# A fused spectral layer and gated MLP: the scaling of the last two table groups given to ScalarE, and the two hand-written orders of the front replaced

## The chip, the cores and the metric

The kernel runs on one core of one Trainium2 chip. The metric is the device time of one execution in microseconds (us), the median over several runs. A profile is one execution seen by the hardware profiler; it counts from the first to the last instruction (the span), which is a little shorter than the device time.

The engines have their own instruction queues and run beside each other: TensorE (PE) multiplies, and its weight loads are listed apart as PEld; VectorE (DVE), ScalarE (ACT) and GpSimd (POOL) work on elements; SyncE (SP) mostly issues DMA transfers. An engine takes its instructions strictly in its program's order, so an instruction that waits for a semaphore holds up everything behind it on that engine.

## What is computed

```python
def _A_ref(x, w_r, w_i):
    X = rfft2(x.astype(float32), axes=(-2, -1))
    X = X * (w_r + 1j * w_i)
    return irfft2(X, s=(S, D), axes=(-2, -1)).astype(bfloat16)

def _B_ref(x, w_gate, w_up, w_down):
    return (gelu(x @ w_gate) * (x @ w_up)) @ w_down

h  = x + _A_ref(layernorm(x), w_r, w_i)      # x: 1 x 2048 x 576, bf16
h2 = h + _B_ref(layernorm(h), w_gate, w_up, w_down)   # F = 4608
```

A layer normalization, a two-dimensional Fourier filter with a residual, a second normalization, and an MLP with a tanh-approximated GELU gate, with a residual.

## The kernel before

**Tiling.** The 2048 tokens are 16 tiles of 128 (partition p, tile c is token 16p+c), each 576 wide, in the SBUF tensor `XO`. The Fourier transforms are matmuls with tables. There are four stages, one after the other in program order.

**Stage 1** (order string `SEQ1`, line 25; from the span's start to about 20 us). The tiles are in six groups, `GROUPS`: tiles 0-1, 2-3, 4-6, 7-9, 10-12, 13-15. For each group the kernel finds the reciprocal deviation of every token (`RS1`), multiplies it into the tables of the first transform (`ATS = ATB * RS1`, `ln1_scale`, line 519 on), and multiplies the tiles with the scaled tables on PE (`a_mm`, line 540 on, 9 matmuls a tile, 18 or 27 a group). A group's matmuls fill five PSUM banks, one after the other, of the eight, in rotation (`a_bank`); the results are copied to the bf16 tensor `U` (`a_ev`, line 556 on). Each word of `SEQ1` emits one step, the last letter being the engine (D = DVE, A = ACT, P = POOL):

- `B3`, `b3`: the two half-row statistics of tile 3 on DVE (L496). Tiles 3, 4 and 13 have their sums from ACT instead: `S` (sum, L488) and `Q` (squares, L492), with `m` a small product (L499).
- `v4`: variances of group 4 on DVE (L505, L508); `q4`: their square root on ACT (L512); `c4`: the reciprocal on DVE (L517), which completes `RS1` of the group.
- `x4`: the scaling of group 4's tables; on DVE one instruction a tile (L527), on POOL one a group (L522).
- `n4`, `t4`: a negated copy (`XN`, L569) and a rearranged tail (`XR`, L576) of the group's tiles, on POOL.
- `k104`: PE matmuls on zeros that only keep PE running (L538). `M4`: the group's matmuls (L553).
- `E22`: the copy of bank-full number 22 (group 22 // 5 = 4, its bank number 22 % 5 = 2 in time) from PSUM to `U` (L564). Bank-fulls named in a word with `F` are copied in two halves: `E` copies the first, which the second stage's first eight steps read, and `F` the second.

**Stage 2** (order string `SEQF`, line 29; about 20 to 47 us). For each of 16 frequency groups i: `Di` and `di` are 6 and 4 matmuls on `U` (L628), and `di`'s letter is the engine that copies the result to `CUS` (L618); `Bq` is 16 matmuls for two groups 2q and 2q+1 (L641); `bi` copies a group's result from PSUM to `YS` (L618); `Ti` multiplies it on DVE with the filter weights (L653), from `YS`, or, where `bi` and `Ti` end in x, from PSUM itself; `Vi` is 16 matmuls (L661) and a copy to `V` (L618); `Zi` gathers a 32-column remainder into `ZR` and `Rq` (8 matmuls, L676) treats the remainders of up to four groups, followed by two DVE instructions into `VR` (L680). A letter at the end of `Z` or `V` is the engine of the copy, ACT where there is none. PSUM is used as four pairs of banks, and `take` (line 600 on) gives each step the pair that has been free longest in the order of the string. So a matmul step waits for the copy that empties its pair.

**Stage 3** (order string `SEQ`, line 30; about 47 to 58 us): inverse transforms (L761, L804), the residual (L821), the second normalization (L828 to L848), transposes (L866) and the first three MLP blocks. It needs all of `V` and `VR`.

**Stage 4** is the MLP: four times 36 blocks of gate and up matmuls (L902, with GELU on ACT L910 and a product on DVE L911), followed by the down matmuls (L1003) and the sum with the residual (L1006). Ten tiles of the inverse transform are woven into the first down pass (L920 to L943).

`Prog.op` records each step with what it reads and writes, and `emit` turns the hazards into semaphore waits. Nothing reorders the steps: each engine's queue is the order of the strings. DMA loads are issued by SP in a fixed order (`LORD`, then the weights); POOL issues some of the MLP's.

Of the kernel before, what the change touches and what calls it, by code (L numbers as in the profile page):

```python
# [6 lines left out]
ACTF = mybir.ActivationFunctionType  # L7
# [14 lines left out]
PAUSE = 600  # L22
PARTS = ((0, 256), (256, 512))
GROUPS = ((0, 2), (2, 4), (4, 7), (7, 10), (10, 13), (13, 16))
SEQ1 = """b1 b0 B0 S3 B1 B2 b2 m3D Q3 v0 q0 c0 t1 v1 k14 q1 n0 S4 t0 Q4 x0D n1 c1 M0 E0D k104 b5 n2 m4P B6 B5 b6 x1P v2 E1A E2A M1 q2 t2 E3A B7 b7 c2 x2P E5A E4A B9 E8A n3 b9 b8 B8 b11 E9A E7A v3 E6A Q13 b14 b10 q3 S13 c3 k202 B11 n4 x3P M2 t3 E12A E11A B10 m13P b12 B12 E10A M3 v4 E14A B14 B15 q4 t4 c4 E13A x4D b15 E16A v5 t5 n5 E15A M4 E18A q5 E17A E19A c5 E20A E24A x5D E21D M5 E25D E23A E22A E26D F24D F26A F23A E28D E27D F28D E29A F25A F29A F22A F27D""".split()
LORD = "x0-2 x2-4 a0-4 x4-8 a4-8 x8-12 x12-16 a8-16".split()
SPLIT = tuple(int(w[1:-1]) for w in SEQ1 if w[0] == "F")
ACT_TILES = tuple(int(w[1:]) for w in SEQ1 if w[0] == "Q")
SEQF = """D1 D0 d1D d0 D3 D2 d3 B0 b0 b1D T1 d2 D4 T0 d4 D5 B1 D6 b2 d5 b3D d6 T3 Z0D V1 Z1P T2 B2 D7 b4 D8 b5 d7D d8 T4 V3 V0 B3 T5 b6 b7 V2 D10 Z2P Z3D Z4D D9 d10 d9 T6 D11 T7 Z5P R0 d11 R1 B4 D13 Z6P b8 T8 b9 Z7D d13 T9 B5 D12 b10 b11 Z8D V4D V5 d12 Z9P T10 R2 D14 D15 d14 V9 d15 Z10P B6 T11 b13D b12 V7 V6 T13 V8 B7 T12 b15 V10 b14x T14x Z11P V11 T15 Z12P V12 V13 Z13P Z14P R3 V14 V15 Z15P R4""".split()
SEQ = """I0 I1 N0 I2 N1 s0 I3 S1 N2 q0 c0 I4 n0 s2 e0 q1 N3 e1 n1 I5 c1 z0 s3 e2 n2 D1 N4 q2 c2 D2 n3 N5 g10 e3 g00 h10 z3 h00 g20 g11 h20 h11 g01 g21 h01 h21""".split()  # L30
QR0 = ((0, 2), (2, 3), (3, 4))
QR = QR0 + ((4, NPRE), (NPRE, 8), (8, 16))
# [294 lines left out]
def _build(nc, A_x, A_w_r, A_w_i, B_w_gate, B_w_up, B_w_down, out):  # L327
    P = Prog(nc)
    T = build_tables()
    dram = {n: nc.inline_tensor(_np_bf16(T[n]), name="c_" + n.lower()) for n in T}  # L330
    PE, DVE, ACT, SP, POOL = "pe", "dve", "act", "sp", "pool"
# [38 lines left out]
    RS1 = sb.alloc("RS1", [128, NT], F32)  # L370
# [30 lines left out]
    ATB = sb.alloc("ATB", [128, NT, 128], BF16)  # L401
    ATS = sb.alloc("ATS", [128, NT, 128], BF16)
# [44 lines left out]
    for i, w in enumerate(LORD):  # L447
        c0, c1 = (int(v) for v in w[1:].rstrip("@").split("-"))
# [46 lines left out]
    def ln1_half(c, h):  # L495
        P.op(DVE, lambda v: v.bn_stats(ST1[:, c, h, :], XO[:, c, 288 * h:288 * h + 288]), r=[("X", c)], w=[("ST1", c, h)])  # L496
# [22 lines left out]
    def ln1_scale(i, eng):  # L519
        c0, c1 = GROUPS[i]  # L520
        if eng == POOL:
            P.op(POOL, lambda g, c0=c0, c1=c1: g.tensor_tensor(ATS[:, c0:c1, :], ATB[:, c0:c1, :],  # L522
                                                               RS1[:, c0:c1].unsqueeze(2).to_broadcast([128, c1 - c0, 128]), op=ALU.mult),
                 r=[("RS1", i)] + [("ATB", c) for c in range(c0, c1)], w=[("ATS", c) for c in range(c0, c1)])
        else:
            for c in range(c0, c1):
                P.op(DVE, lambda v, c=c: v.tensor_scalar(ATS[:, c, :], ATB[:, c, :], RS1[:, c:c + 1], None, op0=ALU.mult),  # L527
                     r=[("RS1", i), ("ATB", c)], w=[("ATS", c)])
# [27 lines left out]
    def a_ev(n, eng, late=False):  # L556
        i, k = n // 5, AORD[n % 5]
        hs = (1,) if late else (0,) if n in SPLIT else (0, 1)
        g0, g1 = 8 * hs[0], 8 * hs[-1] + 8
        c0, c1 = GROUPS[i]  # L560
        m, b = c1 - c0, a_bank(i, k)
        src = bank(b, 0, 128, 0, 128 * m).rearrange("p (n g e) -> p n g e", n=m, g=64)[:, :, 4 * g0:4 * g1, :]
        dst = U[:, k, g0:g1, :, c0:c1, :].rearrange("p g s n e -> p n (g s) e")
        fn = (lambda v: v.tensor_copy(dst, src)) if eng == DVE else (lambda a: a.activation(dst, src, ACTF.Copy))  # L564
        P.op(eng, fn, r=[("PS", b)] + ([("EV", n)] if late else []), w=[("U", i, k, h) for h in hs] + ([] if late else [("EV", n)]))
# [11 lines left out]

    ENG = {"A": ACT, "D": DVE, "P": POOL}
    RUN1 = {"k": idle_mm, "S": act_sum, "Q": act_sq, "B": lambda c: ln1_half(c, 0), "b": lambda c: ln1_half(c, 1), "v": ln1_var, "q": ln1_sqrt, "c": ln1_rs, "M": a_mm, "x": ln1_scale, "E": a_ev, "F": lambda n, eng: a_ev(n, eng, True), "n": x_neg, "m": act_mean2, "t": x_tail}
    for w in SEQ1:  # L580
        a = w[1:]
# [3 lines left out]
    c = 0  # L585
    while c < NT:
        c1 = c + 1
        while c not in ACT_TILES and c1 < NT and c1 not in ACT_TILES:
# [3 lines left out]
             r=[(keys, k) for k in range(c, c1)], w=[("NM", k) for k in range(c, c1)])  # L592
        c = c1
# [152 lines left out]
    for t, w in enumerate(SEQ):  # L746
        k, i = w[0], int(w[1:])
# [326 lines left out]
```

## Time and profile before

| | |
|---|---|
| time, median of 3 runs | 490.08 us (489.91 to 490.16) |
| the profiled execution's own time | 489.97 us |
| its span, granted TensorE clock | 487.7 us, 1.000 |
| PE busy | 479.9 us, 98% of the span |
| DVE busy | 191.6 us, 39% |
| ACT busy | 147.0 us, 30% |
| POOL busy | 33.8 us, 7% |

The busy shares are means over stages that are limited by different things: PE alone counts in the long MLP, while in the first 57 us all engines are busy. The times of rows in the timeline and in the chain of waits are a start and a length in us from the span's start; "x3" is the number of instructions put into the row, and a bracket is the idle time of the engine ahead of it with what ended it. A length includes some latency that the next instruction of the same engine overlaps, so the distance from one start to the next is a little shorter than the length.

### The profile page before, as it was taken

The page shows a single profiled execution, that of the slowest core. Times are in us where ns is not written, and L with a number is a line of the kernel's source. Part 1 is how long each engine was busy: PE and PEld are TensorE (multiplying, and loading weights), DVE is VectorE, ACT ScalarE, POOL GpSimd, SP SyncE. Part 2 cuts the span into 40 slices and gives each one's busy share as a digit, 9 for nine tenths or more (in the row PEclk, how much of TensorE's full clock was granted, in tenths as well). Part 3 has the DMA queues.
Part 4 walks back from the last instruction along what each step waited for, and adds up shares of the span by engine and source line. Part 5 has one row for each costly group of instructions (what it writes and reads, how often), then busy time and mean ns, then how long its engine had stood idle before and what let it go on. Part 6 is the DMA issues. An engine that isn't in the chain of part 4 may idle for free.

```text
span 487.7 us, 10651 instructions
## 1 busy us (share of the span) xinstructions
PE 479.9 (98%) x4725; PEld 281.8 (58%) x4726; DVE 191.6 (39%) x382; ACT 147.0 (30%) x289; POOL 33.8 (7%) x66
## 2 busy tenths in 40 slices
PE   7899999999999999999999999999999999999998
PEld 3667744444688744444577644444677444444775
DVE  6888733433576534333311144333211233333111
ACT  6898733223222222233200022332100123323000
POOL 5412720000000010000000000000000000000000
DMA  8657999300001071100000001000000000000000
GB/s 281 156 146 223 316 354 370 103 13 1 1 22 38 16 234 23 23 1 1 0 19 20 13 21 23 13 1 1 7 19 18 7 1 1 1 1 1 13 18 19
DMA packets 26205, 31.03 MB, mean 64 GB/s; under 512 B 11792, under 2 KB 18320, under 8 KB 26160
## 3 DMA queue, kind: packets, MB, share of 16 engines
q1 hardware_dynamic: 23904, 21.07, 15.1%
q0 software_dynamic: 2256, 9.29, 5.4%
q8 instruction: 37, 0.61, 0.5%
q14 instruction: 8, 0.07, 0.0%
HBM read 26.02 MB, written 2.36 MB: 58 GB/s over the span
## 4 chain that ended last, share of the span: by engine, by line
PE 94%; DVE 3%; DMA 1%; POOL 0%; issue 0%; SPq 0%; ACT 0%; POOLq 0%; DVEq 0%
PE PS L902 57%; PE PS L1003 29%; PE PS L628 2%; PE PS L661 1%; DVE ST L496 1%; DMA XO<-in_A_x_dram 1%; PE PS L920 1%; PE PS L641 1%; DVE VR L680 1%; PE PS L938 1%; DVE XO L821 0%; PE PS L804 0%; PE PS L761 0%; DVE ATS L527 0%; SPq L237 0%
## 5 line engine op out<-in xcount | busy, mean ns | idle before, releaser
L902 PE MATMUL PS<-HT,WG 64*128 64x512 bf16 (+1 forms) x2160 | 228.7, 371 | 0.0
L902 PEld LDWEIGHTS PS<-HT,WG 64*128 64x128 bf16 x2160 | 105.0, 94 | 122.0 <-issue 0.9
L911 DVE TENSOR_TENSOR AT<-GL,PS 128x512 bf16<-128x512 bf16 (+1 forms) x147 | 99.4, 677 | 177.9 <-ACT GL L910 177.9
L910 ACT ACTIVATE GL<-PS 128x512 bf16<-128x512 f32 (+1 forms) x147 | 86.5, 588 | 262.9 <-PE PS L902 251.6
L1003 PE MATMUL PS<-WD,AT 128*128 128x288 bf16 (+2 forms) x1152 | 144.9, 286 | 0.0
L1003 PEld LDWEIGHTS PS<-WD,AT 128*128 128x128 bf16 x1152 | 110.7, 98 | 30.6 <-ACT GL L910 1.3
L902 PE MATMUL PS<-HT,WGX 64*128 64x512 bf16 x486 | 53.4, 376 | 0.0
L1006 DVE TENSOR_TENSOR OS<-PS,XO 128x288 bf16<-128x288 f32 (+2 forms) x32 | 14.6, 457 | 94.4 <-PE PS L1003 94.3
L902 PEld LDWEIGHTS PS<-HT,WGX 64*128 64x128 bf16 x486 | 23.7, 94 | 28.8
L628 PE MATMUL PS<-FT,U 64*128 64x288 bf16 x160 | 12.1, 284 | 0.4 <-ACT U L564 0.3
L925 ACT ACTIVATE EB<-PS 128x288 f32<-128x288 f32 x10 | 4.1, 410 | 27.7 <-PE PS L920 27.7
L553 PE MATMUL PS<-ATS,XO 128*128 128x128 bf16 x96 | 9.1, 220 | 2.6 <-POOL ATS L522 2.1
L653 DVE TENSOR_TENSOR TP<-YS,WS 128x1152 bf16<-128x1152 bf16 x15 | 11.0, 755 | 0.4 <-ACT YS L618 0.2
L496 DVE BATCH_NORM_STATS2 ST<-XO 128x6 f32<-128x288 bf16 x26 | 9.9, 441 | 2.3 <-DMA XO<-in_A_x_dram 2.3
L943 DVE TENSOR_TENSOR XO<-PS,XO 128x576 bf16<-128x576 f32 x10 | 7.6, 757 | 8.0 <-PE PS L938 8.0
L553 PEld LDWEIGHTS PS<-ATS,XO 128*128 128x128 bf16 x96 | 6.8, 98 | 4.9 <-POOL ATS L522 3.3
L931 DVE TENSOR_TENSOR QB<-PS,EB 128x288 f32<-128x288 f32 x20 | 8.2, 452 | 3.3 <-ACT EB L925 3.3
L848 DVE TENSOR_SCALAR HN<-XO,NM,RS 128x576 bf16<-128x576 bf16 (+1 forms) x28 | 9.3, 368 | 0.0
L564 ACT ACTIVATE U<-PS 128x384 bf16<-128x384 f32 (+2 forms) x29 | 9.2, 415 | 0.1
L618 ACT ACTIVATE CUS<-PS 128x576 bf16<-128x576 f32 x14 | 8.8, 657 | 1.4 <-PE PS L628 1.4
L628 PEld LDWEIGHTS PS<-FT,U 64*128 64x128 bf16 x160 | 6.4, 94 | 4.2 <-PE PS L628 0.7
L661 PE MATMUL PS<-VT,TP 64*128 64x128 bf16 x256 | 8.7, 217 | 0.1
(86 smaller groups left out, 203.1 us busy)
## 6 DMA issues: line engine op xcount, KB each, us to landing
WD<-in_B_w_down_dram POOLq DMA_DIRECT2D x9, 576.0 KB, 17.1
WG<-in_B_w_up_dram SPq DMA_DIRECT2D x3, 1152.0 KB, 12.7
WG<-in_B_w_gate_dram POOLq DMA_DIRECT2D x2, 1152.0 KB, 13.1
out_dram<-OS SPq DMA_DIRECT2D x30, 72.0 KB, 1.6
XO<-in_A_x_dram SPq DMA_DIRECT2D x3, 576.0 KB, 7.1
WG<-in_B_w_gate_dram SPq DMA_DIRECT2D x4, 288.0 KB, 3.8
WG<-in_B_w_up_dram SPq DMA_DIRECT2D x4, 288.0 KB, 3.7
WG<-in_B_w_gate_dram SPq DMA_DIRECT2D x1, 1152.0 KB, 9.6
```

Source lines behind the costliest of these rows:

```text
L496: P.op(DVE, lambda v: v.bn_stats(ST1[:, c, h, :], XO[:, c, 288 * h:288 * h + 288]), r=[("X", c)], w=[("ST1", c, h)])
L553: P.op(PE, lambda t, b=b, lhs=lhs, s=s, e=e, o=o, c=c: t.matmul(bank(b, 0, 128, o, o + 128), lhs, ATS[:, c, :], start=s, stop=e), r=[("X", ...
L564: fn = (lambda v: v.tensor_copy(dst, src)) if eng == DVE else (lambda a: a.activation(dst, src, ACTF.Copy))
L628: d_done[i, o] = P.op(PE, lambda t, b=b, us=us, h0=h0, o=o, s=(not second and j == 0), e=(second and j == 1): t.matmul(bank(b, 0, 128, 0, ...
L653: P.op(DVE, lambda v: v.tensor_tensor(TP[:, i % NP, :, :, :], y4, w4, op=ALU.mult), r=rk + wkeys[sum(i >= w[1] for w in WP)], w=[("T", i % ...
L661: P.op(PE, lambda t, c=c, h0=h0, h=h, k=k, vt=vt: t.matmul(bank(b + h, 0, 128, 128 * c, 128 * c + 128), TP[h0:h0 + 64, i % NP, k // 2, k % ...
L848: P.op(eng, lambda v, c=c, hs=hs, o0=o0, o1=o1, x0=x0, x1=x1: v.tensor_scalar(HN[:, hs, o0:o1], XO[:, c, x0:x1], NM[:, c:c + 1], RS2[:, c: ...
L902: op = P.op(PE, lambda t, h0=h0, kt=kt, wt=wt, b=b, s=(not second and j == 0), e=(second and j == n - 1): t.matmul(bank(b, 0, 128, c0, c1) ...
L910: P.op(ACT, lambda a: a.activation(GL[:, s2, c0:c1], bank(b0, 0, 128, c0, c1), ACTF.Gelu_apprx_tanh), r=[("PS", b0)], w=[("GL", s2)])
L911: P.op(DVE, lambda v: v.tensor_tensor(AT[:, f, c0:c1], GL[:, s2, c0:c1], bank(b0 + 1, 0, 128, c0, c1), op=ALU.mult), r=[("GL", s2), ("PS", ...
L1003: P.op(PE, lambda t, b=b, d0=d0, d1=d1, f=f, p=p: t.matmul(bank(b, 0, 128, 0, d1 - d0), AT[:, f, 128 * p:128 * p + 128], WD[:, f, d0:d1], ...
L1006: P.op(DVE, lambda v, b=b, d0=d0, d1=d1, p=p, c=c: v.tensor_tensor(OS[:, p % 2, d0:d1], bank(b, 0, 128, 0, d1 - d0), XO[:, c, d0:d1], op=A ...
```

## The change

Three things change, all of them ahead of stage 3. First, `ln1_scale` gets a branch for ScalarE (one activation a tile: a copy with `RS1` as the per-partition scale), and `SEQ1` uses it for groups 4 and 5, which DVE had (`x4D`, `x5D` become `x4A`, `x5A`); group 0 goes from DVE to GpSimd (`x0D` becomes `x0P`); groups 1 to 3 stay on GpSimd. Second, the copies of the bank-fulls are dealt out anew between ACT and DVE: DVE had nine (`E0`, `E21`, and seven halves) and now has twelve (`E14`, `E17`, `E18`, `E21`, and eight halves); ACT goes from 29 to 26. Third, the whole of both order strings is another order. In `SEQF` the copies of `d3`, `b4`, `V3`, `V8` go from ACT to DVE and those of `V4` and `b1` from DVE to ACT; `Z0`, `Z3`, `Z12` go to ACT, `Z1` to DVE, and `Z4`, `Z7`, `Z8` to GpSimd; `b14x`, `T14x` (the product from PSUM) become `b14`, `T14`. The lines behind line 525 move down by 4: L564 is L568 after the change, L628 is L632, and so on.

```diff
@@ -22,11 +22,11 @@
-SEQ1 =
-    b1 b0 B0 S3 B1 B2 b2 m3D Q3 v0 q0 c0 t1 v1 k14 q1 n0 S4 t0 Q4 x0D n1 c1 M0 E0D k104 b5 n2 m4P B6 B5 b6 x1P v2
-    E1A E2A M1 q2 t2 E3A B7 b7 c2 x2P E5A E4A B9 E8A n3 b9 b8 B8 b11 E9A E7A v3 E6A Q13 b14 b10 q3 S13 c3 k202 B11
-    n4 x3P M2 t3 E12A E11A B10 m13P b12 B12 E10A M3 v4 E14A B14 B15 q4 t4 c4 E13A x4D b15 E16A v5 t5 n5 E15A M4
-    E18A q5 E17A E19A c5 E20A E24A x5D E21D M5 E25D E23A E22A E26D F24D F26A F23A E28D E27D F28D E29A F25A F29A
-    F22A F27D
+SEQ1 =
+    S3 b0 B1 t1 B0 n0 b2 t0 b1 m3D v0 Q3 q0 B2 k14 c0 v1 q1 x0P M0 n1 E1A S4 c1 B5 Q4 b5 B6 k104 n2 m4P E2A b6 v2
+    b7 E0A x1P B7 q2 c2 B9 b8 M1 t2 B8 b9 v3 E5A E4A E3A x2P B11 E6A E7A B12 b10 E8A k202 M2 b11 S13 E11A q3 c3 n3
+    n4 E12A B10 b12 Q13 E10A x3P E9A t3 v4 B14 q4 b15 m13P c4 b14 t4 M3 B15 E13A v5 E15A x4A q5 E14D c5 E16A M4 t5
+    n5 x5A E17D E19A E20A E18D E24A E23D F23A E22A E21D M5 E25D E26D E27A E28D F24A E29D F26A F28D F29D F25A F22D
+    F27A
-SEQF =
-    D1 D0 d1D d0 D3 D2 d3 B0 b0 b1D T1 d2 D4 T0 d4 D5 B1 D6 b2 d5 b3D d6 T3 Z0D V1 Z1P T2 B2 D7 b4 D8 b5 d7D d8 T4
-    V3 V0 B3 T5 b6 b7 V2 D10 Z2P Z3D Z4D D9 d10 d9 T6 D11 T7 Z5P R0 d11 R1 B4 D13 Z6P b8 T8 b9 Z7D d13 T9 B5 D12
-    b10 b11 Z8D V4D V5 d12 Z9P T10 R2 D14 D15 d14 V9 d15 Z10P B6 T11 b13D b12 V7 V6 T13 V8 B7 T12 b15 V10 b14x
-    T14x Z11P V11 T15 Z12P V12 V13 Z13P Z14P R3 V14 V15 Z15P R4
+SEQF =
+    D0 D1 d0 d1D D2 D3 d2 d3D B0 D4 D5 b1 b0 T1 T0 d4 d5 B1 b2 b3D D6 T3 Z0 V0 d6 B2 D7 T2 b5 D8 b4D d7D d8 V2 V1
+    T5 Z1D B3 b7 T4 T7 Z2P D10 D9 b6 d10 d9 Z3 T6 V3D Z4P Z5P D11 Z6P R0 d11 V5 R1 B4 b8 T8 b9 Z7P T9 V4 B5 b10
+    D12 b11 T10 D13 Z8P d12 D14 d13 R2 d14 D15 Z9P d15 V10 B6 T11 b12 b13D V6 T12 V7 B7 T13 b14 Z10P b15 Z11P V8D
+    T14 Z12 V12 Z13P V9 V13 V11 T15 Z14P R3 V14 V15 Z15P R4
@@ -522,6 +522,10 @@
             P.op(POOL, lambda g, c0=c0, c1=c1: g.tensor_tensor(ATS[:, c0:c1, :], ATB[:, c0:c1, :],
                                                                RS1[:, c0:c1].unsqueeze(2).to_broadcast([128, c1 - c0, 128]), op=ALU.mult),
                  r=[("RS1", i)] + [("ATB", c) for c in range(c0, c1)], w=[("ATS", c) for c in range(c0, c1)])
+        elif eng == ACT:
+            for c in range(c0, c1):
+                P.op(ACT, lambda a, c=c: a.activation(ATS[:, c, :], ATB[:, c, :], ACTF.Copy, scale=RS1[:, c:c + 1]),
+                     r=[("RS1", i), ("ATB", c)], w=[("ATS", c)])
         else:
             for c in range(c0, c1):
                 P.op(DVE, lambda v, c=c: v.tensor_scalar(ATS[:, c, :], ATB[:, c, :], RS1[:, c:c + 1], None, op0=ALU.mult),
```

More of the change, by code (lines that the diff above doesn't have):

```diff
@@ L24 @@
 GROUPS = ((0, 2), (2, 4), (4, 7), (7, 10), (10, 13), (13, 16))
-SEQ1 = """b1 b0 B0 S3 B1 B2 b2 m3D Q3 v0 q0 c0 t1 v1 k14 q1 n0 S4 t0 Q4 x0D n1 c1 M0 E0D k104 b5 n2 m4P B6 B5 b6 x1P v2 E1A E2A M1 q2 t2 E3A B7 b7 c2 x2P E5A E4A B9 E8A n3 b9 b8 B8 b11 E9A E7A v3 E6A Q13 b14 b10 q3 S13 c3 k202 B11 n4 x3P M2 t3 E12A E11A B10 m13P b12 B12 E10A M3 v4 E14A B14 B15 q4 t4 c4 E13A x4D b15 E16A v5 t5 n5 E15A M4 E18A q5 E17A E19A c5 E20A E24A x5D E21D M5 E25D E23A E22A E26D F24D F26A F23A E28D E27D F28D E29A F25A F29A F22A F27D""".split()
+SEQ1 = """S3 b0 B1 t1 B0 n0 b2 t0 b1 m3D v0 Q3 q0 B2 k14 c0 v1 q1 x0P M0 n1 E1A S4 c1 B5 Q4 b5 B6 k104 n2 m4P E2A b6 v2 b7 E0A x1P B7 q2 c2 B9 b8 M1 t2 B8 b9 v3 E5A E4A E3A x2P B11 E6A E7A B12 b10 E8A k202 M2 b11 S13 E11A q3 c3 n3 n4 E12A B10 b12 Q13 E10A x3P E9A t3 v4 B14 q4 b15 m13P c4 b14 t4 M3 B15 E13A v5 E15A x4A q5 E14D c5 E16A M4 t5 n5 x5A E17D E19A E20A E18D E24A E23D F23A E22A E21D M5 E25D E26D E27A E28D F24A E29D F26A F28D F29D F25A F22D F27A""".split()
 LORD = "x0-2 x2-4 a0-4 x4-8 a4-8 x8-12 x12-16 a8-16".split()
@@ L28 @@
 ACT_TILES = tuple(int(w[1:]) for w in SEQ1 if w[0] == "Q")
-SEQF = """D1 D0 d1D d0 D3 D2 d3 B0 b0 b1D T1 d2 D4 T0 d4 D5 B1 D6 b2 d5 b3D d6 T3 Z0D V1 Z1P T2 B2 D7 b4 D8 b5 d7D d8 T4 V3 V0 B3 T5 b6 b7 V2 D10 Z2P Z3D Z4D D9 d10 d9 T6 D11 T7 Z5P R0 d11 R1 B4 D13 Z6P b8 T8 b9 Z7D d13 T9 B5 D12 b10 b11 Z8D V4D V5 d12 Z9P T10 R2 D14 D15 d14 V9 d15 Z10P B6 T11 b13D b12 V7 V6 T13 V8 B7 T12 b15 V10 b14x T14x Z11P V11 T15 Z12P V12 V13 Z13P Z14P R3 V14 V15 Z15P R4""".split()
+SEQF = """D0 D1 d0 d1D D2 D3 d2 d3D B0 D4 D5 b1 b0 T1 T0 d4 d5 B1 b2 b3D D6 T3 Z0 V0 d6 B2 D7 T2 b5 D8 b4D d7D d8 V2 V1 T5 Z1D B3 b7 T4 T7 Z2P D10 D9 b6 d10 d9 Z3 T6 V3D Z4P Z5P D11 Z6P R0 d11 V5 R1 B4 b8 T8 b9 Z7P T9 V4 B5 b10 D12 b11 T10 D13 Z8P d12 D14 d13 R2 d14 D15 Z9P d15 V10 B6 T11 b12 b13D V6 T12 V7 B7 T13 b14 Z10P b15 Z11P V8D T14 Z12 V12 Z13P V9 V13 V11 T15 Z14P R3 V14 V15 Z15P R4""".split()
 SEQ = """I0 I1 N0 I2 N1 s0 I3 S1 N2 q0 c0 I4 n0 s2 e0 q1 N3 e1 n1 I5 c1 z0 s3 e2 n2 D1 N4 q2 c2 D2 n3 N5 g10 e3 g00 h10 z3 h00 g20 g11 h20 h11 g01 g21 h01 h21""".split()
```

## Prediction

> **What bounds the kernel now.** I read the chain of waits first, in order of time, and its tail before its front.
>
> ```profile
> 20.47 2.40 PE PS L628 x36
> ...
> 47.24 1.03 PE PS L761 x7
> ...
> 55.72 1.63 PE PS L902 x28
> ...
> 57.74 68.58 PE PS L902 x674
> ...
> 450.04 35.40 PE PS L1003 x288
> ```
>
> From 57.74 on the chain is PE behind PE to the end, so the MLP is neither shortened nor lengthened here, and its matmuls follow each other without a gap. What the change can move is when the chain reaches 57.74. Stage 3 (47.24 to 57.74) keeps its order, so it moves as a block with the last L680 instruction, which ends at 47.2. Everything is decided in the two stretches ahead of it; the windows view gives their load.
>
> ```profile
> core 0: us, PE busy (x) PEld busy (x) DVE busy (x) ACT busy (x) POOL busy (x), PEclk, DMA share, GB/s
> 3.65:20.47 16.82, 13.88 (x159) 9.56 (x159) 15.73 (x65) 13.92 (x45) 11.39 (x23) 1.00 0.84 250
> 20.47:44.67 24.20, 23.98 (x552) 17.28 (x554) 20.38 (x37) 21.91 (x43) 4.29 (x10) 1.00 0.63 171
> ```
>
> In stage 1 DVE is busy 15.73 of 16.82 us and ACT 13.92 (94% and 83%): DVE is the fullest, ACT next. In stage 2 PE is busy 23.98 of 24.20 and ACT 21.91, so work given to ACT there has little room. A gain would be of the size of a us at most, 0.2% of the time; 0.2% (0.98 us) is also about what a measurement of this kernel can tell from no change.
>
> **Stage 1, step by step.** The walk below takes each engine's queue in the new order, the start-to-start distances of these rows, and the hops that they show.
>
> ```profile
> 9.05 0.61 POOL L522 TENSOR_TENSOR ATS<-ATB,RS 128x256 bf16<-128x256 bf16 x1
> ...
> 10.79 0.83 POOL L522 TENSOR_TENSOR ATS<-ATB,RS 128x384 bf16<-128x384 bf16 x1 [0.56 <-DVE RS L517]
> ...
> 13.76 0.83 POOL L522 TENSOR_TENSOR ATS<-ATB,RS 128x384 bf16<-128x384 bf16 x1 [0.17 <-POOL XN L569]
> ```
>
> ```profile
> 6.57 0.17 DVE L517 RECIPROCAL RS<-RS 128x2 f32<-128x2 f32 x1 [0.36 <-ACT RS L512]
> ...
> 10.49 0.16 DVE L517 RECIPROCAL RS<-RS 128x3 f32<-128x3 f32 x1
> 10.57 1.87 DVE L496 BATCH_NORM_STATS2 ST<-XO 128x6 f32<-128x288 bf16 x5
> ...
> 13.29 0.16 DVE L517 RECIPROCAL RS<-RS 128x3 f32<-128x3 f32 x1
> ...
> 15.99 0.83 DVE L527 TENSOR_SCALAR ATS<-ATB,RS 128x128 bf16<-128x128 bf16 x3
> ...
> 17.87 0.18 DVE L517 RECIPROCAL RS<-RS 128x3 f32<-128x3 f32 x1 [0.36 <-ACT RS L512]
> 18.08 0.58 DVE L527 TENSOR_SCALAR ATS<-ATB,RS 128x128 bf16<-128x128 bf16 x3
> ```
>
> ```profile
> 10.09 2.01 ACT L564 ACTIVATE U<-PS 128x256 bf16<-128x256 f32 x7
> 11.93 0.73 ACT L492 ACTIVATE JNK<-XO 128x576 bf16<-128x576 bf16 x1
> ...
> 13.59 1.62 ACT L564 ACTIVATE U<-PS 128x384 bf16<-128x384 f32 x4
> ...
> 17.54 0.30 ACT L512 ACTIVATE RS<-MV,EPT 128x3 f32<-128x3 f32 x1 [0.56 <-DVE MV L508]
> 17.74 3.48 ACT L564 ACTIVATE U<-PS 128x384 bf16<-128x384 f32 x12
> ...
> 50.14 0.77 ACT L795 ACTIVATE OS<-XO,NM 128x576 bf16<-128x576 bf16 x1
> ```
>
> ```profile
> 7.16 0.23 PE L553 MATMUL PS<-ATS,XO 128*128 128x128 bf16 x1 [0.26 <-DVE ATS L527]
> ...
> 9.72 0.23 PE L553 MATMUL PS<-ATS,XO 128*128 128x128 bf16 x1 [0.47 <-POOL ATS L522]
> ...
> 14.65 0.23 PE L553 MATMUL PS<-ATS,XO 128*128 128x128 bf16 x1 [1.30 <-POOL ATS L522]
> ...
> 19.79 0.39 PE L553 MATMUL PS<-ATS,XO 128*128 128x128 bf16 x4
> ```
>
> *Removed from DVE*: two scalings of group 0 and one copy of it (0.34 net), 0.83 for group 4 and 0.58 for group 5. *Added to DVE*: three full copies (`E14`, `E17`, `E18`) and one half more, all behind the last statistics.
>
> *Group 0.* One statistic (1.87 / 5 = 0.36 in distance) now stands behind the group's variances, so its reciprocal, at 6.57 before, comes at 6.21. GpSimd starts 0.14 behind the reciprocal's end and takes 0.61: 6.52 to 7.13, and PE starts at 7.19 (7.16 before). Nothing gained or lost.
>
> *What stands behind it on GpSimd*: `n1`, `n2`, `m4`, `x1`. They move back by 0.61 and a gap of 0.15, less idle time; `x1` starts at 9.47 (9.05), M1 at 10.14 (9.72), and ScalarE, whose next copy now needs M1, idles from 10.19 to 10.58. `x2` is cheap: it had 0.56 idle ahead of it, and with `t2` ending at 10.65 it starts at 10.8, as before.
>
> *Reciprocals of groups 2 and 3.* ScalarE now copies `E1` before it reads tile 4, so the squares that DVE needs are done at 9.6, and DVE idles 0.3; the reciprocal of group 2 comes at 10.44 (10.49). Between it and group 3's there are now eight statistics where there were seven, so that comes at 13.67 (13.29). Hence `x3` at 13.97 (13.76) and M3 at 14.86 (14.65).
>
> *The new scalings.* No row shows ScalarE on a 128-wide SBUF tile with a per-partition operand. Its nearest rows are 0.30 for 3 elements and 0.77 for 576 (L512 and L795, both with such an operand). On the line between them 128 elements take 0.40, and as the next instruction overlaps 0.10 (17.54 + 0.30 against the start at 17.74), some 0.31 lie from start to start. The ends are 0.20 (what the three-element row leaves, 17.54 to 17.74) and 0.40 (no overlap). I take 0.31, the line between its two rows: 0.93 a group, 1.86 in all, where DVE gave 1.41. The Trainium skill, "ScalarE: Activation LUTs", section "Rules for kernel authors", says to do a multiplication on VectorE and not on ScalarE; section "What ACT_TABLE_LOAD costs" has 186 ns + 93 ns for the operand + 0.833 ns an element, 93 ns of it overlapped, 0.29 a tile by an estimate from that, which would make the sum 0.1 less; no run here shows it yet.
>
> *ScalarE's queue* is then full. From 10.58: six 256-wide copies (0.263 apart: seven of them stand between 10.09 and 11.93), the sum of tile 13 (0.66), `E11`, square root 3, `E12`, squares of 13, `E10`, `E9`, square root 4, `E13`, `E15` (0.39 for each 384-wide one, 0.20 for a root) give 16.12. `x4`: 16.12 to 17.05. Root 5 and `E16`: 17.64. `x5`: 18.57. So group 4's third tile is ready at 17.14 (DVE: 16.82), group 5's at 18.66 (18.66): the earlier last reciprocal (17.39, before 17.87) is spent in ScalarE's queue: behind `x4`, which itself waits behind `E15` for PE, stand root 5, `E16` and `x5`, and for these wait DVE's reciprocal and M5. M5, 27 matmuls behind that tile and behind the copies that empty its banks, ends at 20.17 (20.18): no change.
>
> *The tail of the copies.* Behind `x5` ScalarE has `E19`, `E20` (0.79) and eight halves.
>
> ```profile
> 19.77 1.45 ACT L564 ACTIVATE U<-PS 128x192 bf16<-128x192 f32 x6
> ```
>
> At 0.23 each (1.45 less the last one's overlap, over six), `F24`, the fourth from the end, ends at 20.6, `F25` at 21.07. They free PSUM banks 1 and 2. In the new order the second matmul of `D0` writes bank 1 and the first of `D1` bank 2, so `D1` starts at 21.13. Before, the second D step began at 20.47 + 0.39 = 20.86, with 2.40 / 36 for a matmul. **Stage 1 costs 0.27 us.** Below, with 0.20 a scaling, it gains 0.4; with 0.40 it costs 0.8.
>
> **Stage 2.** The matmuls are the same 584. I walked the new order with 0.39 for a D step, 0.25 for d, 0.62 for B, 0.45 for V, and copies as below.
>
> ```profile
> 22.79 0.68 PE L641 MATMUL PS<-CUS,BT 64*64 64x288 bf16 x16
> 23.41 1.64 PE L628 MATMUL PS<-FT,U 64*128 64x288 bf16 x20
> ...
> 39.48 0.80 PE L641 MATMUL PS<-CUS,BT 64*64 64x288 bf16 x16
> ...
> 42.38 2.02 PE L661 MATMUL PS<-VT,TP 64*128 64x128 bf16 x64
> ```
>
> ```profile
> 32.43 1.76 ACT L618 ACTIVATE CUS<-PS 128x576 bf16<-128x576 f32 x3
> ...
> 43.13 3.07 ACT L618 ACTIVATE V<-PS 128x512 bf16<-128x512 f32 x6
> ```
>
> ```profile
> 41.19 1.43 DVE L653 TENSOR_TENSOR TP<-YS,WS 128x1152 bf16<-128x1152 bf16 x2
> 42.54 1.35 DVE L653 TENSOR_TENSOR TP<-PS,WS 128x1152 bf16<-128x1152 f32 x1
> ...
> 44.66 2.52 DVE L680 TENSOR_TENSOR VR<-PS,MK 128x512 bf16<-128x512 f32 x4
> ```
>
> ACT has 0.55 between 576-wide copies and 0.50 between 512-wide ones, and a dependent engine starts 0.1 to 0.17 behind an end. Two `B` steps mark the way: the first starts at 23.30 (22.79 before; D2 and d2 now stand ahead of it, so 0.25 of that is order), the seventh at 39.9 (39.48, with the same number of D and V steps ahead). The shift stays between 0.25 and 0.6, because ScalarE's load (22 us in 24) and the bank pairs hold PE to the same pace. The end gains a little: `T14` no longer reads PSUM (1.35 becomes 0.75), though `V8`'s copy (0.69) joins DVE's queue just ahead of it, and the last four DVE products run in the same 3.4 us. The last L680 ends at 47.38 (47.19): **0.2 us later in all**; stage 2 gives 0.1 back.
>
> The cover of what I put at nothing: the weight loads of the MLP. SP's order is unchanged, GpSimd's weight transfers stand behind the same last `Z15`, and the one PE instruction that it waits for before the first up weights is again in the middle of a V step (`V7` instead of `V6`, both behind `B6`).
>
> ```profile
> 41.26 4.48 SPq L237 DMA_DIRECT2D WG<-in_B_w_up_dram  x5
> ```
>
> ```profile
> WG<-in_B_w_up_dram SPq DMA_DIRECT2D x4, 288.0 KB, 3.7
> ```
>
> Issued by 45.74 and landing 3.7 later, they are there by 50, over 5 us before the first gate matmuls at 55.72.
>
> **The sum**: profiled execution 489.97 + 0.2 = 490.2; the median of the runs is 0.1 above that execution, so 490.3.
>
> **The rivals.**
>
> *Faster: DVE's relief counts in full.* If a scaling on ScalarE is 0.20 and ScalarE's copies start a few tenths earlier than I walked, M5 ends 0.6 sooner, at 19.6, and the last half copies with it; D1 then starts at 20.4, 0.45 early. If stage 2 also keeps the 0.67 that DVE loses on `T14`, the sum is 490.1 - 1.1 = 489.0. For it: DVE is the fullest engine of stage 1, its last reciprocal surely comes earlier, and half of the chain's pieces there are DVE's. Against it: ScalarE gets 1.86 us and has 16.82 - 13.92 = 2.9 to spare, most of it at moments when it has nothing ready.
>
> *Slower: ScalarE becomes the bound of stage 1.* Its queue has no idle time from 10.58 to the end; `x4` stands behind `E15`, and square root 5, which group 5 waits for, behind `x4`. Each 0.1 more for a scaling is 0.6 in the tail copies and in the first D steps. At 0.40 with a M1 that is another 0.2 late, stage 1 costs 1.0, and stage 2, with ScalarE the fullest engine next to PE, gives nothing back and loses 0.2 at bank pairs: 491.3. It decides from a scaling of about 0.38. The rule of the skill quoted above points here.
>
> *No effect at all*: that the front's time is hidden behind a weight load. The loads land 5 us early, so I give this nothing beyond the forecast's own middle.
>
> **How the numbers follow.** The forecast (both engines' changes cancel, 489.1 to 491.0) has 0.57; faster by over 0.2% has 0.17; slower by over 0.2% 0.26, more than faster since ScalarE's queue has no slack and the walk already ends late. The range of 8 in 10 runs from the faster case to the slower one: 489.0 to 491.4.
>
> **What would show it.** ScalarE's L527 rows at 0.40 each, 0.93 for three; the last reciprocal at 17.4; GpSimd's first L522 at 6.5 and the second at 9.5; M3's first matmul at 14.9; the first L632 matmuls (L628 before) from 20.4 with a stall for a U copy of ScalarE, 36 of them until 23.3; the last L684 ending at 47.4; the MLP's unbroken stretch from 57.9. A last L684 before 46.4 would make the prediction wrong, and show that stage 2 is paced by DVE; one behind 48.2 that ScalarE holds the front.

## The result, and the profile after

| | before | after |
|---|---|---|
| time, median of 21 runs each | 489.95 us (489.77 to 490.67) | 489.20 us (489.08 to 489.52) |
| ratio, with its 95% interval | | 0.9984 [0.9977, 0.9990] |
| the profiled execution's own time, its span | 489.97, 487.7 | 489.13, 487.3 |
| time outside the span | 2.24 | 1.80 |

The change makes the kernel 0.75 us faster, 0.16%: less than the 0.2% that the prediction took as the least that can be told, and yet told, since 21 runs give an interval that leaves out 1. The forecast was 0.2 us slower. The last row of the table is the mean, over the runs, of the time less the span of the same run (for the kernel before it was 2.22 to 2.24 in each batch of the experiments). It splits the gain: 0.3 us lie within the span (median 487.4, before 487.7), **0.44 us lie outside it**, in a place for which the prediction has no term at all.

The chain of waits of the changed kernel, in order of time (start, length, engine and line; lines behind 525 are 4 higher than before):

```profile
13.80 0.84 POOL ATS L522
...
14.69 1.68 PE PS L557 x27
...
16.39 0.28 PE PS L557 x2
...
16.68 0.28 PE PS L557 x2
...
16.96 3.07 PE PS L557 x50
...
20.27 2.71 PE PS L632 x39
...
22.98 0.61 PE PS L645 x16
...
42.29 0.65 ACT YS L622
...
43.14 2.94 ACT V L622 x6
...
46.21 1.68 PE PS L765 x12
...
57.37 68.58 PE PS L906 x674
```

Two things differ from the chain before. In stage 1 it ran through VectorE's statistics, scalings and copies, and two copies on ScalarE, until 20.47; at the end of stage 2 it ran through VectorE's last four products (L680). Its rows before the change:

```profile
18.08 0.58 DVE ATS L527 x3
18.66 1.09 DVE U L564 x3
19.77 0.56 ACT U L564 x2
...
46.62 0.57 DVE VR L680
```

Now stage 1 is PE behind PE from M3's start at 14.69 on, because the scalings of groups 4 and 5 are there, or nearly there, when PE comes to them: PE's weight loads wait 0.17 to 0.19 for each of group 4's three tiles (two matmuls to a tile in the rows at 16.39 and 16.68), and for group 5's the waits list none.

At the end of stage 2 the chain runs through ScalarE's last six copies of `V`, by a thin margin: five matmuls wait for these copies and start at 46.21, and when they are through, at some 46.85, VectorE's products have just ended too (44.33 + 2.47 = 46.80).

```profile
44.33 2.47 DVE L684 TENSOR_TENSOR VR<-PS,MK 128x512 bf16<-128x512 f32 x4
...
46.86 0.30 PE L765 MATMUL PS<-DT,VR 128*128 128x288 bf16 x1
```

The MLP's unbroken stretch starts at 57.37 (57.74), and nothing changes behind that.

The windows of stages 1 and 2 (busy time of PE, PEld, DVE, ACT, POOL):

```profile
3.65:20.47 16.82, 14.47 (x163) 9.85 (x161) 15.16 (x59) 14.53 (x50) 11.92 (x24) 1.00 0.79 244
20.47:44.67 24.20, 24.13 (x561) 17.43 (x559) 21.29 (x35) 21.70 (x43) 5.34 (x12) 1.00 0.60 175
```

VectorE gives 0.57 in stage 1, ScalarE takes 0.61 more, and PE, with 14.47 for 13.88, is done with more of its work by 20.47. The timelines of single engines show the steps that the prediction walked. VectorE's last two reciprocals, of groups 4 and 5:

```profile
15.31 0.18 DVE L517 RECIPROCAL RS<-RS 128x3 f32<-128x3 f32 x1
...
17.13 0.18 DVE L517 RECIPROCAL RS<-RS 128x3 f32<-128x3 f32 x1
```

ScalarE's two groups of scalings and the tail of its copies:

```profile
15.84 1.06 ACT L527 ACTIVATE ATS<-ATB,RS 128x128 bf16<-128x128 bf16 x3
16.71 0.38 ACT L512 ACTIVATE RS<-MV,EPT 128x3 f32<-128x3 f32 x1
16.90 0.58 ACT L568 ACTIVATE U<-PS 128x384 bf16<-128x384 f32 x1
17.34 1.00 ACT L527 ACTIVATE ATS<-ATB,RS 128x128 bf16<-128x128 bf16 x3
18.23 2.66 ACT L568 ACTIVATE U<-PS 128x384 bf16<-128x384 f32 x10
```

Three scalings take 0.87 from start to start (15.84 to 16.71) and 0.89 (17.34 to 18.23), 0.29 each. The weight loads of the first D steps:

```profile
19.96 0.09 PEld L632 LDWEIGHTS PS<-FT,U 64*128 64x128 bf16 x1
20.27 2.41 PEld L632 LDWEIGHTS PS<-FT,U 64*128 64x128 bf16 x39 [0.22 <-ACT U L568]
```

D starts at 19.96 (20.47), and its second matmul waits 0.22 for a copy of `U` on ScalarE.

### The profile page after: what moved, and what is told of

Same layout as the page of the kernel before. It is cut to its first block, busy times and chain, and to the rows that moved or that the text cites. A ratio compares the mean times of both kernels' runs of the same rounds, so it can differ in the third digit from the quotient of the medians.

```text
span 487.3 us, 10655 instructions
## 1 busy us (share of the span) xinstructions
PE 480.2 (99%) x4726; PEld 281.7 (58%) x4726; DVE 191.7 (39%) x375; ACT 147.4 (30%) x294; POOL 35.2 (7%) x68
## 4 chain that ended last, share of the span: by engine, by line
PE 96%; DVE 2%; ACT 1%; issue 0%; POOL 0%; POOLq 0%; DVEq 0%
PE PS L906 58%; PE PS L1007 29%; PE PS L632 2%; PE PS L542 1%; PE PS L557 1%; PE PS L924 1%; PE PS L645 1%; DVE ST L496 1%; PE PS L665 1%; ACT V L622 1%; PE PS L942 1%; PE PS L765 0%; DVE XO L825 0%; PE PS L808 0%; PE PS L870 0%
## 5 line engine op out<-in xcount | busy, mean ns | idle before, releaser
L632 PE MATMUL PS<-FT,U 64*128 64x288 bf16 x160 | 12.2, 284 | 0.1
L568 ACT ACTIVATE U<-PS 128x256 bf16<-128x256 f32 (+2 forms) x26 | 8.9, 449 | 1.2 <-PE PS L557 1.2
L542 PE MATMUL PS<-ZD 128*128 128x512 bf16 x20 | 7.4, 537 | 1.5 <-POOL ZD L430 1.5
L632 PEld LDWEIGHTS PS<-FT,U 64*128 64x128 bf16 x160 | 6.4, 94 | 4.2 <-ACT CUS L622 0.7
```

Source lines behind the costliest of these rows:

```text
L542: P.op(PE, lambda t: t.matmul(bank(b), ZD[:, 0:128], ZD[:, :], start=True, stop=True), r=["ZD"], w=[("PS", b)])
L632: d_done[i, o] = P.op(PE, lambda t, b=b, us=us, h0=h0, o=o, s=(not second and j == 0), e=(second and j == 1): t.matmul(bank(b, 0, 128, 0, ...
```

## The experiments

Each was timed in five rounds on the chip, with the kernel before beside it (489.93 to 490.02 in the five batches). "Span" is the median over a kernel's runs, "outside" the mean of time less span, and VectorE's count is the one of the profile page.

| kernel | time | span | outside | VectorE's count |
|---|---|---|---|---|
| before, with the branch unused (c0_control) | 489.97 | 487.7 | 2.23 | 382 |
| after | 489.20 | 487.4 | 1.80 | 375 |
| new `SEQ1`, old `SEQF` (s1_seq1_new) | 489.47 | 487.7 | 1.79 | 377 |
| old `SEQ1`, new `SEQF` (s2_seqf_new) | 489.62 | 487.5 | 2.12 | 380 |
| after, groups 4 and 5 on VectorE (x45d_new_order) | 490.61 | 488.6 | 2.03 | 381 |
| before, groups 4 and 5 on ScalarE (x45_old_order) | 491.33 | 489.5 | 1.80 | 376 |
| after, group 0 on VectorE (x0d_new_order) | 489.33 | 487.5 | 1.82 | 377 |
| after, group 3 on VectorE (after_x3_vector) | 489.77 | 487.9 | 1.82 | 378 |
| after, 0.28 us more in ScalarE's queue (x5_twice) | 489.48 | 487.7 | 1.80 | 375 |
| after, tail copies in another order (tail_swapped) | 489.20 | 487.4 | 1.81 | 375 |
| after, T14 from PSUM (after_t14_from_psum) | 490.57 | 488.8 | 1.79 | 375 |
| before, T14 in two steps (before_t14_two_step) | 491.07 | 488.9 | 2.14 | 382 |
| before, six VectorE memsets fewer (before_six_fewer_dve) | 489.49 | 487.6 | 1.87 | 376 |
| before, two VectorE memsets fewer (before_three_fewer_dve) | 489.81 | 487.7 | 2.10 | 380 |
| after, eight VectorE memsets more (after_eight_more_dve) | 489.66 | 487.5 | 2.15 | 383 |
| after, 32 VectorE memsets more (after_32_more_dve) | 489.29 | 487.5 | 1.81 | 407 |
| after, eight ScalarE instructions more (after_eight_more_act) | 489.22 | 487.4 | 1.81 | 375 |

**The theory at the start**: the new orders gain by taking the last scalings off VectorE. **Its rivals**: the gain is stage 2's alone, or it is no matter of the schedule at all.

### Which string carries it

```diff
 c0_control:   the branch of ln1_scale added, both strings as before
 s1_seq1_new:  SEQ1 as after, SEQF as before
 s2_seqf_new:  SEQ1 as before, SEQF as after
```

> The kernel before with the new branch of ln1_scale in the source and unused: the same instructions in the same order, four source lines lower. Both theories: 489.95 +- 0.15 us, ratio 1.000. It asks something else: the profiled executions differ by 0.84 us in time (489.97, 489.13) but by 0.4 in span (487.7, 487.3), so 0.4 lies outside the span. If that is a chance of the one execution of before, this kernel's executions have spans near 488.1 and 1.85 us outside; if it belongs to the kernel, spans near 487.7 and 2.25 us outside.

> The new SEQ1 (with ScalarE's scalings) and the old SEQF. Theory A (stage 2's order gave most of the gain: in the traces the first D step starts 0.5 earlier but the stalls behind it leave 0.12 of stage 1's gain, and 0.26 comes from stage 2): time 489.8 us, and the last L684 ends at 47.1. Theory B (stage 1 gave it all, stage 2's order only passes it on): 489.2 us, last L684 at 46.8.

> The old SEQ1 and the new SEQF. Theory A (stage 2's order is itself 0.26 us shorter, above all by the product T14 that no longer reads PSUM): 489.6 us, last L684 near 46.9. Theory B (stage 2's order only fits the new end of stage 1): 489.95 us or slower, since D0 and D1 then write the banks whose copies come last in the old order (up to 490.3).

The control has ratio 0.9999 [0.9991, 1.0008] and the same 2.23 outside: that part belongs to a kernel and not to chance. The new `SEQ1` alone gives 0.9991 [0.9982, 0.9999], nearly all of it outside: the last L684 ends at 47.10 as theory A had it (before: 47.18), and the time is lower than its 489.8 because of the part outside, which neither theory counted. Its chain of waits still ends stage 2 in VectorE:

```profile
22.84 0.61 PE PS L645 x16
...
44.64 0.69 DVE VR L684
```

The new `SEQF` alone gives 0.9994 [0.9985, 1.0003], by itself not told from no change, at theory A's 489.6; its chain passes through ScalarE's copies, as in the changed kernel:

```profile
43.35 2.94 ACT V L622 x6
...
57.57 68.58 PE PS L906 x674
```

So the shift of the chain at the end of stage 2 is `SEQF`'s work, worth 0.2 us of span. The two gains, 0.49 and 0.34, add up to about the 0.75 of both. Within the span the new `SEQ1`, with its scalings taken off VectorE, gives nothing that can be told beside the old `SEQF` (487.7) and 0.1 beside the new (487.5 to 487.4). That leaves little of the theory at the start: 0.44 of the 0.75 lies outside the span, and 0.2 is stage 2's.

### The scalings, in the new order and in the old

```diff
 x45d_new_order (from after):
-x4A ... x5A
+x4D ... x5D
 x45_old_order (from before):
-x4D ... x5D
+x4A ... x5A
 x0d_new_order (from after):
-x0P
+x0D
```

> The new orders with groups 4 and 5 scaled by VectorE (x4D, x5D) at the same places of the string. Theory A (the move to ScalarE is worth nothing by itself, the orders are): 489.2 +- 0.2 us. Theory B (the move relieves VectorE, which is the fullest engine of stage 1): VectorE has 1.4 us more behind its reciprocals, of which the copies E17, E18, E23, E21 behind them are late: M5's banks come free 0.5 to 1 late, 490.0 us.

> The kernel before with its own orders, and only the scalings of groups 4 and 5 given to ScalarE. Theory 'the new orders are what makes room for them': ScalarE's old queue has no room, B's first step comes 0.3 to 0.9 later than 22.79, 490.2 to 490.8. Rival 'the relief of VectorE pays by itself': B's first step up to 0.5 earlier, 489.4 to 489.8. VectorE's count falls only by what the scalings take away, so outside the span 2.0 to 2.24.

> The changed kernel with group 0's scalings back on VectorE. Theory 'giving group 0 to POOL frees VectorE for the later groups, and only the last third of a chain decides': VectorE is 0.5 us later from there on, D's first step 0.2 to 0.5 later than 19.96, 489.3 to 489.6. Rival 'ScalarE paces stage 1 from 10.6 on, VectorE has slack': 489.2, no change.

In the new order, VectorE in place of ScalarE costs 1.2 us of span: 1.0013 [1.0004, 1.0023] of before, in theory B's direction and nearly twice its size. VectorE's timeline there shows why: the last reciprocal, which stood at 17.13, comes at 18.11, behind group 4's scalings, and D starts at 21.15 (19.96).

```profile
16.50 1.24 DVE L531 TENSOR_SCALAR ATS<-ATB,RS 128x128 bf16<-128x128 bf16 x3
...
18.11 0.16 DVE L517 RECIPROCAL RS<-RS 128x3 f32<-128x3 f32 x1
```

In the old order, the same edit the other way costs 1.8 us of span: 1.0028 [1.0017, 1.0038], more than the 490.2 to 490.8 that the first theory had. There ScalarE's timeline has four copies between square root 5 and `x5`, which starts only at 19.47 (17.34 in the changed kernel), and M5 waits 1.36 for it:

```profile
17.96 0.29 ACT L512 ACTIVATE RS<-MV,EPT 128x3 f32<-128x3 f32 x1
18.15 1.47 ACT L568 ACTIVATE U<-PS 128x384 bf16<-128x384 f32 x4
19.47 1.01 ACT L527 ACTIVATE ATS<-ATB,RS 128x128 bf16<-128x128 bf16 x3
```

So the engine of the scalings and the order belong together: each undone alone is worse than both kernels. Group 0's engine hardly matters: 489.33, with a spread of runs (488.97 to 489.65) that covers 489.20 and does not decide between the two expectations.

### Is there slack left in stage 1?

```diff
 x5_twice (from after), behind the scalings of group 5 on ScalarE:
+for c in range(c0, c1):
+    activation(TM[:, 1, c:c+1], ATB[:, c, 0:1], Copy)
 tail_swapped (from after):
-E27A E28D F24A E29D F26A F28D F29D F25A
+F24A E27A E28D E29D F25A F28D F29D F26A
 after_x3_vector (from after):
-x3P
+x3D
```

> The changed kernel with three tiny ScalarE instructions more (some 0.2 to 0.3 us each) behind group 5's scalings. Theory 'ScalarE's queue is full to the end of stage 1, each us in it is a us of the span': 0.6 to 0.8 slower, 489.8 to 490.0. Rival 'B's first step waits for VectorE's or TensorE's work there': within 0.2 of 489.2.

> The changed kernel with ScalarE's tail copies in another order (each F half ahead of the E half before it). Theory 'D's eight steps, which start at 19.96 and last 3.02, wait for the banks that those F halves fill': the stretch shortens by 0.1 to 0.3, 488.9 to 489.1. Rival 'they wait for the last copy of all, whatever its place': 489.2, or up to 0.2 more where an E half comes late.

> The changed kernel with group 3's scalings on VectorE (three of some 0.2 to 0.25 us, M3 can start after the first) in place of POOL's one of 0.83. M3 starts some 0.7 earlier than 14.69, and VectorE is 0.6 to 0.75 later with the statistics and reciprocals of groups 4 and 5. Theory 'from M3's start on TensorE is the pace': D's first step and the end 0.3 to 0.7 earlier, 488.5 to 488.9. Rival 'TensorE only waits less where VectorE and ScalarE just keep up, so that the later statistics come back as a wait ahead of M4 or M5': 489.2 to 489.8. VectorE then has 378 instructions on the page, so outside the span 1.8 to 2.1.

The label x5_twice promises more than the edit does: the three instructions took 0.28 of ScalarE's queue, from 18.31 to 18.59, not the 0.6 to 0.8 that the expectation worked with.

```profile
18.31 0.38 ACT L531 ACTIVATE TM<-ATB 128x1 f32<-128x1 bf16 x3
18.59 2.64 ACT L571 ACTIVATE U<-PS 128x384 bf16<-128x384 f32 x10
```

They cost 0.28 (489.48 against 489.20), more than the rival's 0.2: at this place ScalarE has no slack, and what is put into its queue is added to the time. `tail_swapped` (`F24` one place earlier, `F25` and `F26` exchanged) gives 489.20, no change, as its rival had it. The wait ahead of the second D matmul gets shorter by 0.06, the end does not: the loads take 2.46 in place of 2.41, and B's first step starts at 22.88 in place of 22.92, with D's start 0.03 earlier too.

```profile
20.18 2.46 PEld L632 LDWEIGHTS PS<-FT,U 64*128 64x128 bf16 x39 [0.16 <-ACT U L568]
```

`after_x3_vector` (489.77, in its rival's range) did not do what it was made for. In VectorE's order the scalings stand behind two statistics, and start at 14.45, so M3 starts at 14.75, not earlier; but all that follows on VectorE is later.

```profile
13.74 0.79 DVE L496 BATCH_NORM_STATS2 ST<-XO 128x6 f32<-128x288 bf16 x2
14.45 0.81 DVE L531 TENSOR_SCALAR ATS<-ATB,RS 128x128 bf16<-128x128 bf16 x3
15.19 0.34 DVE L505 BATCH_NORM_AGGREGATE MV<-ST 128x2 f32<-128x12 f32 x3
```

Those 0.74 (14.45 to 15.19) cost 0.5 us of span: group 4's reciprocal, its scalings on ScalarE and M4 come later in turn (M4 at 16.96, 16.39 in the changed kernel). So VectorE has 0.2 of slack at most here and ScalarE, at the place of x5_twice, none; PE, which is the chain, has only the small waits for ScalarE shown above. Whether an earlier M3 would help was not tried by it and stays open.

### T14, in the new order and in the old

```diff
 after_t14_from_psum (from after):
-b14 ... T14
+b14x ... T14x
 before_t14_two_step (from before):
-b14x ... T14x
+b14 ... T14
```

> The changed kernel with the product T14 again read from PSUM by VectorE, as before the change. Theory 'stage 2 is paced by VectorE there, and the shorter T14 is its gain': 0.3 to 0.6 slower, 489.5 to 489.8, with the last L684 later by as much. Rival 'stage 2's end is set by ScalarE and by the order in which V is written': 489.2, within 0.1 of the changed kernel.

> The kernel before with its old orders, and the product T14 in two steps (ScalarE copies to SBUF, VectorE multiplies from there) in place of one from PSUM. Theory 'the shorter VectorE step alone is stage 2's gain': the last L680 ends 0.3 to 0.6 ahead of 47.18, 489.4 to 489.7. Rival 'the two-step form needs the order around it, since it puts 0.65 of a copy into ScalarE's queue ahead of the last copies of V': 490.0 to 490.5, and the chain then passes through ScalarE. VectorE's count stays, so outside stays at 2.24.

Both are over a us slower than the kernel they come from, and slower than either of their expectations: 1.0011 [1.0002, 1.0020] of before for the first (489.20 would be 0.9984), 1.0022 [1.0013, 1.0031] for the second. In the first, the chain of waits goes back through VectorE, as before the change:

```profile
42.83 1.36 DVE TP L657
...
44.23 0.62 PE PS L665 x16
...
45.13 0.69 DVE VR L684
...
47.64 1.52 PE PS L765 x11
```

The last L684 ends 0.8 later, and stage 3's matmuls, five of which ran at 46.21 while VectorE was still at its products, nearly all stand behind 47.64. In the second, ScalarE's queue gets the copy `b14`, and VectorE waits 1.65 for the copy of `YS`:

```profile
43.81 0.66 ACT L618 ACTIVATE YS<-PS 128x576 bf16<-128x576 f32 x1
...
44.34 2.99 ACT L618 ACTIVATE V<-PS 128x512 bf16<-128x512 f32 x5
...
44.50 1.43 DVE L653 TENSOR_TENSOR TP<-YS,WS 128x1152 bf16<-128x1152 bf16 x2 [1.65 <-ACT YS L618]
```

The new order gives the copy of `V8` to VectorE, which makes room for it; that this is all that it needs was not tried. The theory that the shorter T14 is stage 2's gain by itself falls: the two-step form is worth 1.4 us of span in the new order and costs 1.2 us in the old.

### The part outside the span

The first five kernels showed 2.23, 2.12 and 2.03 outside with 382, 380 and 381 VectorE instructions, and 1.80 with 375 and 377. GpSimd's count (66 to 68) did not go with it; ScalarE's went the other way (288 to 291 with the long part, 292 and 294 with the short), a rival that two later kernels rule out (289 with 1.87 in before_six_fewer_dve, 294 with 2.15 in after_eight_more_dve). Hence the theory that VectorE's instructions beyond some 377 cost time outside the span, against the rival that it is something else in the new strings.

```diff
 before_six_fewer_dve, before_three_fewer_dve (from before; the second: two of the six only):
-P.op(DVE, memset(EXQ)); P.op(DVE, memset(MK)); 4 x P.op(DVE, memset(MK[32 rows]))
+P.op(POOL, ...) for the same
 after_eight_more_dve, after_32_more_dve (from after, at the start):
+for j in range(8): P.op(DVE, memset(TM[:, 1, j:j+1], 0.0))
 after_eight_more_act (from after, at the start):
+for j in range(8): P.op(ACT, activation(TM[:, 1, j:j+1], EPT, Copy))
```

> The kernel before with six of VectorE's memsets (of EXQ and MK, at the start) given to GpSimd; VectorE then has 434 recorded instructions in place of 440, and nothing else changes. Theory 'the part outside the span goes by VectorE's instruction count': the span stays at 487.7 and what lies outside it falls from 2.24 to about 1.85, so 489.55. Rival 'the part outside hangs on something else in the new orders': 489.96, no change. A third case, that GpSimd's or another engine's count matters as much: 489.96 or more.

> The kernel before with two of VectorE's memsets given to GpSimd (the one of EXQ and the last one of MK); VectorE has 380 instructions on the page in place of 382. Theory 'a slope of some 0.1 us for each VectorE instruction above some 377': outside the span 2.0 to 2.1 in place of 2.24, so 489.75 to 489.85. Rival 'a step': 2.24 and 490.0, or 1.8 and 489.55.

> The changed kernel with eight tiny VectorE memsets more, at the start while VectorE waits for the first transfer; VectorE then has 440 recorded instructions. Theory 'VectorE's count sets the part outside the span': span 487.3 to 487.4 as before, outside 2.25 in place of 1.82, so 489.6. Rival: 489.2, no change.

> The changed kernel with eight tiny ScalarE instructions more, at the start while ScalarE waits; ScalarE then has 454 to 457 recorded instructions, VectorE 432 as in the changed kernel. Theory 'VectorE's count sets the part outside the span': 489.2, no change. Rival 'any engine's instructions do it': 489.6.

> The changed kernel with 32 tiny VectorE memsets at the start, most of them while VectorE waits for the first transfer; 407 VectorE instructions on the page in place of 375. Theory 'a slope without an end, 0.06 to 0.1 each above some 377': outside the span 3.6 to 4.8. Rival 'a ceiling': outside at most 2.3. The memsets may also hold up the first statistics, which shows in the span (some 32 times 0.06, less the wait that ends at 3.5), so outside is what is compared, not the time.

The label of the second says three, the edit moves two. The first four came as the theory had it, within 0.1 us. The line of busy times on the profile's page shows the counts (the last entry of each engine). Before:

```profile
PE 479.9 (98%) x4725; PEld 281.8 (58%) x4726; DVE 191.6 (39%) x382; ACT 147.0 (30%) x289; POOL 33.8 (7%) x66
```

Before with six VectorE memsets fewer, which GpSimd has:

```profile
PE 480.0 (98%) x4726; PEld 281.9 (58%) x4726; DVE 191.1 (39%) x376; ACT 147.0 (30%) x289; POOL 34.3 (7%) x72
```

The changed kernel with eight more:

```profile
PE 480.5 (99%) x4726; PEld 281.8 (58%) x4726; DVE 191.8 (39%) x383; ACT 147.3 (30%) x294; POOL 35.2 (7%) x68
```

The changed kernel with 32 more:

```profile
PE 480.2 (99%) x4726; PEld 281.7 (58%) x4726; DVE 192.1 (39%) x407; ACT 147.3 (30%) x294; POOL 35.2 (7%) x68
```

Six memsets given to GpSimd, with the strings untouched, take 0.37 off the part outside (2.24 to 1.87) and 0.5 off the time: 0.9990 [0.9981, 1.0000], two thirds of what the whole change brought. The six scalings taken off VectorE in the old orders (x45_old_order, 376) do the same to it: 1.80, where 2.0 to 2.24 was expected. Eight VectorE memsets put back 0.35 (1.80 to 2.15); eight ScalarE instructions put back nothing. But **with 32 more VectorE memsets it is 1.81 again**, where a slope without an end asked for 3.6 to 4.8 and a ceiling for up to 2.3. So the slope falls, and so does a ceiling at which more instructions keep the part long: it is not the number as such. In these kernels 380 to 383 go with a long part, 375 to 378 and 407 with a short one. Whether what counts is where VectorE's program ends up with that number was not tried; the cause stays open. The profile lists an instruction transfer about 1 us behind the span's end in before, the control and three other kernels, but it is there with 1.87 outside (before_six_fewer_dve) and not there with 2.15 (after_eight_more_dve), so it is not that transfer.

## Why the prediction was wrong, point by point

- **The walk of stage 1 up to M5 was right.** The first tile landed 0.14 earlier in this execution (statistics from 3.51, 3.65 before), and with 0.14 added the rows stand where the walk put them, to 0.03 up to M3: POOL's first L522 6.38 (6.52 forecast), its second 9.31 (9.47), M3 14.69 (14.86), the last reciprocal 17.13 (17.39, 0.12 off). The shift wears off on the way, though: in after_eight_more_act, the same front with the tile 0.10 later, D starts only 0.04 later.
- **The price of a scaling was nearly right**: 0.29, taken as 0.31. The estimate from the Trainium skill, "ScalarE: Activation LUTs", section "What ACT_TABLE_LOAD costs", was 0.29, and the rows agree. The Trainium skill, "ScalarE: Activation LUTs", section "Rules for kernel authors", sends a multiplication to VectorE and not to ScalarE, since VectorE is faster per element. In price the rows agree with it: from start to start the six scalings took 1.25 on VectorE before the change (15.99 to 16.74, 18.08 to 18.58) and 1.76 on ScalarE behind it. As a rule for their place it does not hold in the new order (1.2 us of span slower on VectorE) and holds in the old (1.8 slower on ScalarE): here it goes by the room in the queues.
- **"Stage 1 costs 0.27 us" failed by the size of its last term.** The wait is the one forecast, the second matmul of D0 for a half copy of ScalarE. But ScalarE's tail starts at 18.23, not 18.57 (0.10 of that are the scalings; of the landing it is less than 0.14, since after_eight_more_act, 0.10 later there, has its tail 0.05 later; the rest is the walk). So PE waits 0.22, and the second matmul comes at 20.27, where the forecast had the D step behind it at 21.13, after a second wait that the row does not show. B's first step is at 22.92, forecast 23.30; with the 0.25 of order that the prediction itself named, stage 1 gains 0.1 (22.92 - 22.79 - 0.25) where it was to lose 0.26. Part of that 0.1 is the landing: beside the old `SEQF` (s1_seq1_new, the tile 0.03 later than before) the first B is at 22.77, only 0.02 earlier.
- **"Stage 2 gives 0.1 back" failed in its middle, and not at its end.** The seventh B came at 39.33, forecast 39.9. The step that failed is "the shift stays between 0.25 and 0.6". The new order puts four matmuls more ahead of the first B (40 weight loads in the rows above, 36 matmuls before), and as their number in all is the same, four fewer stand behind it. From the first B to the seventh it takes 16.41 (before 16.69, forecast 16.6): the 0.25 of order came back whole in that stretch, where the walk let 0.1 come back. The end was right: from the seventh B to the end of the last L684 it is 7.47 (46.80 - 39.33), forecast 7.48, before 7.70. `s2_seqf_new` has the same 16.42 and 7.46, and its 0.2 us of span are this end. The prediction kept VectorE as the end of the chain; ScalarE's copies of `V` now end it, with VectorE beside them. Stage 3 moved as a block, as forecast (10.57 from the last L684 to the MLP, 10.56 before). The two B steps in the changed kernel:

```profile
22.92 0.68 PE L645 MATMUL PS<-CUS,BT 64*64 64x288 bf16 x16
...
39.33 0.69 PE L645 MATMUL PS<-CUS,BT 64*64 64x288 bf16 x16
```

- **The sum had no term outside the span.** "Profiled execution 489.97 + 0.2" took the 2.24 outside as fixed. It fell by 0.44, and of the 1.1 between forecast and time that is two fifths; nearly all of the rest are the two points above (47.38 - 46.80 = 0.58). Six memsets moved show that most of this part can be had with no change to the schedule.
- **The rival "DVE's relief counts in full" (489.0)** came nearest in size, by another way: M5 did not end at 19.6 (its last matmuls start at 19.19 and end at 20.03), and VectorE's 0.67 on T14 is not a saving that stands by itself. That the time lies near this rival is luck: 0.44 of the way there came from outside the span, of which it says nothing.
- **The rival "ScalarE becomes the bound"** had its ground: no slack (x5_twice). Its price, 0.40 a scaling, did not come.

## What to carry to other kernels

An order found for a set of costs is one object with them: one edit put back alone (the scalings, T14) cost 1.2 to 1.8 us either way, though the whole differs by 0.3 us of span, so such a run measures the fit and not the edit. When a step is moved ahead of a mark, what it adds there is missing behind the mark: a walk has to carry both. And when tenths of a us count, the time outside the span is a term of its own: compare time less span for both kernels before explaining the difference by the trace.

## What the runs showed of the hardware that was not expected

The time outside the span is fixed for a program (2.22 to 2.24 us for the kernel before, by batch) but not the same for all: 1.79 to 1.87 us in eleven of the kernels of the table, 2.03 to 2.23 in the six with 380 to 383 VectorE instructions on the page. Neither eight instructions more on ScalarE (1.81) nor six more on GpSimd (1.87) raised it, and 32 more on VectorE (407) left it at 1.81. No page of the profile shows it: it is only in the difference of the two numbers that each run gives. Why some programs have the long part and others the short one stays open.
